# The attention of a fused kernel wholly in plain float32, a pair of heads in two halves of the array

## The chip, the cores and the metric

The kernel runs on one core of one Trainium2 chip. Its time is the device time of one execution in microseconds; the time before is 933.35 us, the median of three runs (932.42 to 933.69).

TensorE multiplies matrices from SBUF into PSUM; each matmul has a weight load, which the profile shows as an engine of its own, PEld. ScalarE (ACT) does activations and copies, VectorE (DVE) elementwise work, and SyncE (SP) issues all transfers.

## The reference

Four batches of 448 rows pass through sigmoid attention (12 heads of 64), then a block with a time shift, a squared ReLU and a gate, then a mixer over rows and channels:

```
scores = q @ k.T / sqrt(64) - log(448)
x   = sigmoid(scores) @ v                      # per head, then the heads side by side: 448 x 768
xk, xr = mu * x + (1 - mu) * x_prev            # x_prev: x shifted by one row
y   = sigmoid(xr @ w_r) * (relu(xk @ w_k)**2 @ w_v)
u   = y + (relu(y.T @ w_tok1) @ w_tok2).T
out = u + relu(u @ w_ch1) @ w_ch2
```

## The kernel before

**Split numbers.** Nearly every product is done on pairs of rounded float32r values. `split` (lines 100 to 105) makes `hi`, a rounded copy (a CAST on ACT or DVE, as the table `ONDVE` says), and `lo = src - hi` (a subtraction on DVE). A product is then three rounded matmuls, hi x hi, hi x lo and lo x hi (`products`, lines 421, 423, 424).

**Attention, per head.** Two heads make a pair, six pairs a batch. `unit_k` and `unit_q` split keys, queries and values of a head. The head dimension is 64, so a K tile holds hi in one half of the 128 rows and lo in the other, and the scores of a chunk of 128 keys are two rounded matmuls over all rows (lines 194, 195), eight for a head. Line 201 is the sigmoid of two chunks. Lines 207 to 215 split it, and the values are seven rounded matmuls (lines 232, 234), with hi and lo of the values side by side in the columns, which line 237 adds.

Twelve heads of the table `NATIVE`, eight in batch 0 and four in batch 1, take the values another way: the sigmoid and the values stay plain float32, and four plain matmuls with 64 columns (line 227) make the head's output; the last has only 64 rows (`TAIL`). `TAIL` is the last chunk of the 448 keys.

**What runs beside what.** Batch 0's attention runs first, with the first weights prepared beside it (after unit number `EARLY`). From then on the units of the next batch's attention stand between the projections: `spread` gives each unit a due time, and `run` takes the units that are due after every two steps of a product. Each weight chunk is loaded, narrowed from float64 on first use (`narrow`, two ACT and two DVE instructions, lines 272 to 281), stored for later use, and split; `w_tick` does so some chunks ahead. A list scheduler then sets the order on each engine by readiness.

**Waits around the units.** `ps_sc` has two buffers of two PSUM banks (scores), `ps_av` one (values). Keys have one buffer, queries, values and plain sigmoids two or three.

Of the kernel before, what the change touches and what calls it, by code (L numbers as in the profile page):

```python
# [9 lines left out]
F32 = mybir.dt.float32  # L10
# [12 lines left out]
P = 128  # L23
# [11 lines left out]
    return ap.bitcast(F32)  # L35


ONDVE = [('K', 0), ('K', 1), ('K', 2), ('K', 3), ('Q', 0), ('Q', 2), ('Q', 3), ('V', 1), ('V', 2), ('kk', 0), ('kk', 3), ('mix', 1), ('mix', 2), ('mix', 3), ('prev', 2), ('sq', 2)]


WARM = 12
END_1 = 1.0
BEG_2 = 0.15
END_2 = 0.65
EARLY = 20

TURNED = 2
TURN = 1
BLK = 32

NATIVE = {(0, 1), (0, 7), (0, 4), (1, 1), (0, 3), (1, 8), (1, 4), (0, 6), (0, 2), (0, 5), (1, 9), (0, 11)}


def native(b, pr, h):
    return (b, 2 * pr + h) in NATIVE


@with_exitstack
def kernel(
# [23 lines left out]
    def pool(name, bufs, **kw):  # L86
        return ctx.enter_context(tc.tile_pool(name=name, bufs=bufs, **kw))
# [2 lines left out]
    wraw, wpool, wsplit = pool("wraw", 3), pool("wpool", 2), pool("wsplit", 3)  # L90
    dram = pool("dram", 1, space=bass.MemoryType.DRAM)
    tmps = pool("tmps", 4)
    a1, a2, a3 = pool("a1", 1), pool("a2", 2), pool("a3", 3)
    ps_mm = pool("ps_mm", 3, space=PSUM)
    ps_av, ps_sc = pool("ps_av", 1, space=PSUM), pool("ps_sc", 2, space=PSUM)

    def ENG(kind, b):
        return DVE if (kind, b) in ONDVE else ACT
# [10 lines left out]

    kns, qns, vns = {}, {}, {}  # L110


    def load_k(g):
        if g < B * NPAIR:
            kns[g] = a1.tile([P, 4 * P], F32, tag="kn", name="kn")
            SP.dma_start(out=kns[g], in_=k[g])

    def load_q(g):
        if g < B * H:
            qns[g] = a2.tile([P, S], F32, tag="qn", name="qn")  # L120
            SP.dma_start(out=qns[g], in_=q[g])

    def load_v(g):
        if g < B * NPAIR:
            vns[g] = a2.tile([P, 2, 4, D], F32, tag="vn", name="vn")
            SP.dma_start(out=vns[g], in_=v[g])


# [7 lines left out]
    for _ in range(WARM):  # L136
        PE.matmul(idle[:, :S], zero[:, :P], zero, start=True, stop=True)

    load_k(0)
    load_q(0)  # L140
    load_v(0)
    load_q(1)

    ident = const.tile([P, P], F32, tag="ident", name="ident")
    make_identity(nc, ident)

    load_v(1)

    mus = {}
    for name, src in (("k", mu_k), ("r", mu_r)):  # L150
# [9 lines left out]

    att = {}

    def unit_k(b, pr, h):
        g = b * NPAIR + pr
        kn = kns[g]
        me = slice(h * D, h * D + D)
        ot = slice(D - h * D, P - h * D)
        K = a3.tile([P, 4 * P], F32R, tag="KK", name="KK")
        split(K[me], K[ot], kn[me], ENG("K", b))
        att[(b, pr, h)] = {"K": K}  # L170

    def unit_q(b, pr, h):
        g = b * NPAIR + pr
        st = att[(b, pr, h)]
        qn = qns.pop(2 * g + h)
        Q1 = a2.tile([P, S], F32R, tag="Q1", name="Q1")
        Q2 = a2.tile([P, S], F32R, tag="Q2", name="Q2")
        split(Q1, Q2, qn, ENG("Q", b))
        st["Q"] = (Q1, Q2)
        vn = vns[g][:, h]  # L180
        if native(b, pr, h):
            st["v"] = vn
        else:
            vs = a3.tile([P, 4, 2 * D], F32R, tag="vs", name="vs")
            split(vs[:, :, 0:D], vs[:, :, D:], vn, ENG("V", b))
            st["v"] = vs

    def unit_qk(b, pr, h, c2):
        st = att[(b, pr, h)]
        K, (Q1, Q2) = st["K"], st["Q"]  # L190
        ps = ps_sc.tile([P, 2, 512], F32, tag="sc", name="psc")
        for j in range(2):
            c = c2 * 2 + j
            PE.matmul(ps[:, j, :S], K[:, c * P : (c + 1) * P], Q1, start=True, stop=False)  # L194
            PE.matmul(ps[:, j, :S], K[:, c * P : (c + 1) * P], Q2, start=False, stop=True)  # L195
        plain = native(b, pr, h)
        if plain:
            a = a3.tile([P, 2, S], F32, tag="al" if c2 else "ah", name="a")
        else:
            a = a2.tile([P, 2, S], F32, tag="a", name="a")  # L200
        ACT.activation(a, ps[:, :, :S], AF.Sigmoid, bias=-math.log(S), scale=1.0 / math.sqrt(D))  # L201
        if plain:
            st[c2] = a
            return
        ah = a3.tile([P, 2, S], F32R, tag="ah", name="ah")
        al = a3.tile([P, 2, S], F32R, tag="al", name="al")
        if ENG("ah", b) is ACT:
            ACT.copy(ah, a)  # L208
        else:
            DVE.tensor_copy(ah, a)  # L210
        if c2 == 0:
            DVE.tensor_tensor(out=al, in0=a, in1=f32(ah), op=ALU.subtract)
        else:
            DVE.tensor_tensor(out=al[:, 0], in0=a[:, 0], in1=f32(ah[:, 0]), op=ALU.subtract)
            DVE.tensor_tensor(out=ah[TAIL:, 1], in0=a[TAIL:, 1], in1=f32(ah[TAIL:, 1]), op=ALU.subtract)  # L215
        st[c2] = (ah, al)

    def unit_av(b, pr, h):
        st = att.pop((b, pr, h))
        vs = st["v"]  # L220
        ps = ps_av.tile([P, 512], F32, tag="av", name="pav")
        me = slice(h * D, h * D + D)
        ot = slice(D - h * D, P - h * D)
        if native(b, pr, h):
            for c in range(4):
                n = P if c < 3 else TAIL
                PE.matmul(ps[:D, :S], vs[:n, c], st[c // 2][:n, c % 2], start=(c == 0), stop=(c == 3))  # L227
            ACT.copy(xe[me, pr, 1:], ps[:D, :S])
            return
        for c in range(4):  # L230
            ah, al = st[c // 2]
            PE.matmul(ps[:, :S], vs[:, c], ah[:, c % 2], start=(c == 0), stop=(c == 3))  # L232
            if c < 3:
                PE.matmul(ps[:, :S], vs[:, c], al[:, c % 2], start=False, stop=False)  # L234
        tmp = tmps.tile([P, S], F32, tag="tmp", name="avt")
        ACT.copy(tmp[me], ps[ot, :S])
        DVE.tensor_tensor(out=xe[me, pr, 1:], in0=ps[me, :S], in1=tmp[me], op=ALU.add)

    def attention_units(b, then=()):

        u = [lambda: unit_k(b, 0, 0), lambda: unit_q(b, 0, 0), lambda: unit_k(b, 0, 1)]
        for pr in range(NPAIR):
            nx = pr + 1 < NPAIR
            u.append(lambda pr=pr: (unit_qk(b, pr, 0, 0), load_q(2 * (b * NPAIR + pr) + 2)))
            if pr == 0:
                u.append(lambda: load_k(b * NPAIR + 1))
            u.append(lambda pr=pr: unit_q(b, pr, 1))
            if pr:
                u.append(lambda pr=pr: (unit_av(b, pr - 1, 1), load_v(b * NPAIR + pr + 1)))
                u += [f[pr - 1] for f in then]  # L250
            u.append(lambda pr=pr: (unit_qk(b, pr, 0, 1), load_q(2 * (b * NPAIR + pr) + 3)))
            if nx:
                u.append(lambda pr=pr: unit_k(b, pr + 1, 0))
            u.append(lambda pr=pr: unit_qk(b, pr, 1, 0))
            u.append(lambda pr=pr: unit_av(b, pr, 0))
            if nx:
                u.append(lambda pr=pr: unit_q(b, pr + 1, 0))
                u.append(lambda pr=pr: unit_k(b, pr + 1, 1))
            u.append(lambda pr=pr, nx=nx: (unit_qk(b, pr, 1, 1), nx and load_k(b * NPAIR + pr + 2)))
        u.append(lambda: (unit_av(b, NPAIR - 1, 1), load_v(b * NPAIR + NPAIR + 1)))  # L260
        u += [f[NPAIR - 1] for f in then]
        return u

# [417 lines left out]
def lay_out(x):  # L681

    import numpy as np

    def chunks(w, parts=1):

        kt = w.shape[0] // (P * parts)
        w = w.reshape(parts, kt, P, w.shape[1] // P, P).transpose(3, 0, 2, 1, 4)
        return w.reshape(-1, P, kt * P)

    qt = x["q"].transpose(0, 1, 3, 2).reshape(B * H, D, S)
    kt = x["k"].transpose(0, 1, 3, 2).reshape(B * NPAIR, P, S)
    v = x["v"].reshape(B * NPAIR, 2, S, D)
    head = v[:, :, : 3 * P].reshape(B * NPAIR, 2, 3, P, D).transpose(0, 3, 1, 2, 4)
    tail = v[:, :, 3 * P :].transpose(0, 2, 1, 3)[:, :, :, None]
    y = {
        "q": np.concatenate([qt, qt], axis=1),
        "k": np.concatenate([kt, kt[:, :, 3 * P :]], axis=2),
        "v": np.concatenate([head, np.concatenate([tail, tail], axis=1)], axis=3),
        "moe_mu_k": x["moe_mu_k"].reshape(NT, P).T,  # L700
        "moe_mu_r": x["moe_mu_r"].reshape(NT, P).T,
        "moe_w_k": chunks(x["moe_w_k"]),
        "moe_w_v": chunks(x["moe_w_v"], 2),
        "moe_w_r": chunks(x["moe_w_r"]),
        "moe2_w_tok1": chunks(np.concatenate([x["moe2_w_tok1"], x["moe2_w_tok1"][3 * P :]])),
        "moe2_w_tok2": x["moe2_w_tok2"],
        "moe2_w_ch1": chunks(x["moe2_w_ch1"]),
        "moe2_w_ch2": chunks(x["moe2_w_ch2"], 2),
    }
    y = {n: np.ascontiguousarray(a) for n, a in y.items()}  # L710

    return {n: a.view(np.int64) if a.dtype == np.float64 else a for n, a in y.items()}
# [41 lines left out]
```

## Time and profile before

| | |
|---|---|
| median of three runs | 933.35 us |
| span of the profiled execution (the page gives no other time for it) | 933.1 us |
| TensorE matmuls busy | 919.8 us, 99% |
| weight loads busy | 803.6 us, 86% |
| VectorE busy | 663.0 us, 71% |
| ScalarE busy | 518.2 us, 56% |
| transfers, share of 16 engines | 46.2% |

A matmul's record lasts longer than the step to the next, since matmuls are pipelined: busy time says that TensorE had work, and the distance of two starts says what a matmul costs. A "128*64" ahead of a matmul's shape is the part of the array that it takes, rows by columns.

### The profile page before, as it was taken

Reading aid. Unit: us, or ns where it says so; the run is one execution under the profiler, and the core shown is the slowest. Engines: PE = TensorE matmul, PEld = TensorE weight load, DVE = VectorE, ACT = ScalarE, POOL = GpSimd, SP = SyncE. Lnnn points to the kernel's source line nnn. Section 1 sums busy time; section 2 is a strip of 40 time slices with the busy share of each in tenths; the row PEclk is TensorE's granted clock in tenths of the full one; section 3 lists DMA queues with packets and bytes.
Section 4 is the critical chain, followed back from the end, with each engine's and each line's share of the span. In section 5 each row is a group of like instructions: output and inputs, shape, how many; then the busy total and the mean of one; then the engine's idle time right before and its main releaser. Section 6 shows DMA issues by size and latency. Waiting matters only on the chain.

```text
span 933.1 us, 12192 instructions
## 1 busy us (share of the span) xinstructions
PE 919.8 (99%) x4448; PEld 803.6 (86%) x4448; DVE 663.0 (71%) x1117; ACT 518.2 (56%) x794; POOL 1.3 (0%) x10
## 2 busy tenths in 40 slices
PE   8999999999999999999999999999999999999998
PEld 3477888789999889899898999999999999898987
DVE  7999999998567998677889379988745552332231
ACT  6998998864665867545641277766444432112210
POOL 0000000000000000000000000000000000000000
PEclk9999999999999999999999999999999999999999
DMA  7844866754446656565534333343335421242131
GB/s 250 274 137 129 291 233 199 229 170 129 117 124 192 228 170 198 174 221 194 171 137 152 130 115 115 107 123 95 109 105 161 126 81 51 81 136 71 51 101 72
DMA packets 63228, 138.77 MB, mean 149 GB/s; under 512 B 12736, under 2 KB 29632, under 8 KB 63168
## 3 DMA queue, kind: packets, MB, share of 16 engines
q1 hardware_dynamic: 63168, 137.99, 46.2%
q8 instruction: 35, 0.57, 0.2%
q14 instruction: 25, 0.20, 0.1%
HBM read 106.96 MB, written 29.62 MB: 146 GB/s over the span
## 4 chain that ended last, share of the span: by engine, by line
PE 86%; DVE 8%; DMA 4%; issue 1%; ACT 1%; SPq 0%; ACTq 0%; DVEq 0%
PE psmm L424 24%; PE psmm L421 24%; PE psmm L423 23%; PE pav L227 4%; PE psc L194 3%; PE psc L195 3%; PE pav L232 2%; DMA raw<-in_moe_w_ch_dram 2%; PE pav L234 2%; DVE wlo L105 1%; DMA raw<-in_moe_w_r_dram 1%; DVE wd L280 1%; DVE wd L277 1%; DMA kn<-in_k_dram 1%; PE psmm L474 1%
## 5 line engine op out<-in xcount | busy, mean ns | idle before, releaser
L424 PE MATMUL psmm<-Ah,wlo 128*128 128x448 f32 (+2 forms) x688 | 248.9, 362 | 0.5 <-DVE wlo L105 0.5
L421 PE MATMUL psmm<-Ah,whi 128*128 128x448 f32 (+2 forms) x688 | 248.8, 363 | 0.0
L102 ACT CAST whi<-wd 128x768 fp32r<-128x768 f32 (+1 forms) x160 | 121.6, 760 | 222.6 <-PE psmm L423 210.4
L423 PE MATMUL psmm<-Al,whi 128*128 128x448 f32 (+2 forms) x672 | 243.5, 362 | 0.1
L105 DVE TENSOR_TENSOR wlo<-wd,whi 128x768 fp32r<-128x768 f32 (+1 forms) x160 | 137.8, 861 | 88.5 <-ACT whi L102 86.3
L421 PE MATMUL psmm<-Mh,whi 128*128 128x448 f32 (+2 forms) x480 | 175.7, 366 | 0.0
L423 PE MATMUL psmm<-Ml,whi 128*128 128x448 f32 (+2 forms) x480 | 174.8, 364 | 0.8 <-DVE Ml L105 0.8
L424 PE MATMUL psmm<-Mh,wlo 128*128 128x448 f32 (+2 forms) x480 | 174.9, 364 | 0.0
L421 PEld LDWEIGHTS psmm<-Ah,whi 128*128 128x128 f32 x688 | 129.2, 188 | 14.2 <-issue 2.8
L424 PEld LDWEIGHTS psmm<-Ah,wlo 128*128 128x128 f32 x688 | 129.2, 188 | 11.6 <-DVE wlo L105 0.9
L423 PEld LDWEIGHTS psmm<-Al,whi 128*128 128x128 f32 x672 | 126.2, 188 | 11.9 <-DVE Al L105 0.8
L201 ACT ACTIVATE a<-psc 128x896 f32<-128x896 f32 x96 | 87.4, 916 | 22.6 <-PE psc L195 22.1
L423 PEld LDWEIGHTS psmm<-Ml,whi 128*128 128x128 f32 x480 | 90.2, 188 | 9.8 <-DVE Ml L105 1.1
L421 PEld LDWEIGHTS psmm<-Mh,whi 128*128 128x128 f32 x480 | 90.2, 188 | 9.3 <-issue 0.7
L424 PEld LDWEIGHTS psmm<-Mh,wlo 128*128 128x128 f32 x480 | 90.1, 188 | 8.6
L195 PE MATMUL psc<-Q,KK 128*128 128x448 f32 x192 | 70.2, 367 | 1.3 <-DVE Q L105 1.3
L194 PE MATMUL psc<-Q,KK 128*128 128x448 f32 x192 | 70.8, 371 | 0.7 <-ACT a L201 0.4
L208 ACT CAST ah<-a 128x896 fp32r<-128x896 f32 x72 | 67.8, 943 | 1.3
L274 ACT ACTIVATE raw<-raw 128x768 uint32<-128x768 uint32 (+2 forms) x54 | 45.5, 842 | 30.8 <-DMA raw<-in_moe_w_ch_dram 25.1
L272 ACT ACTIVATE wd<-raw 128x768 f32<-128x768 f32 (+2 forms) x54 | 45.1, 836 | 20.0 <-DVE wlo L105 16.3
L277 DVE SCALAR_TENSOR_TENSOR wd<-wd,raw 128x768 uint32<-128x768 uint32 (+2 forms) x54 | 46.9, 872 | 10.2 <-ACT wd L272 9.8
L232 PE MATMUL pav<-ah,vs 128*128 128x448 f32 x144 | 53.6, 372 | 0.2 <-DVE ah L215 0.2
(85 smaller groups left out, 1031.1 us busy)
## 6 DMA issues: line engine op xcount, KB each, us to landing
wd<-w SPq DMA_DIRECT2D x66, 384.0 KB, 3.0
raw<-in_moe_w_ch_dram SPq DMA_DIRECT2D x24, 768.0 KB, 5.3
w<-wd SPq DMA_DIRECT2D x38, 384.0 KB, 2.7
qn<-in_q_dram SPq DMA_DIRECT2D x48, 224.0 KB, 3.0
wd<-w SPq DMA_DIRECT2D x42, 256.0 KB, 2.8
kn<-in_k_dram SPq DMA_DIRECT2D x24, 256.0 KB, 2.8
vn<-in_v_dram SPq DMA_DIRECT2D x24, 256.0 KB, 3.8
raw<-in_moe_w_k_dram SPq DMA_DIRECT2D x8, 768.0 KB, 6.6
```

What stands on the lines that cost most here:

```text
L102: ACT.copy(hi, src)
L105: DVE.tensor_tensor(out=lo, in0=src, in1=hi.bitcast(F32), op=ALU.subtract)
L194: PE.matmul(ps[:, j, :S], K[:, c * P : (c + 1) * P], Q1, start=True, stop=False)
L195: PE.matmul(ps[:, j, :S], K[:, c * P : (c + 1) * P], Q2, start=False, stop=True)
L201: ACT.activation(a, ps[:, :, :S], AF.Sigmoid, bias=-math.log(S), scale=1.0 / math.sqrt(D))
L208: ACT.copy(ah, a)
L232: PE.matmul(ps[:, :S], vs[:, c], ah[:, c % 2], start=(c == 0), stop=(c == 3))
L274: ACT.activation(lo, lo, AF.Copy, bias=0.4375, scale=0.875 * 2.0**-29)
L277: DVE.scalar_tensor_tensor(out=dst, in0=dst, scalar=3, in1=lo, op0=ALU.logical_shift_left, op1=ALU.bitwise_or)
L421: PE.matmul(ps[:, :n], wh, xh, start=(i == 0), stop=False)
L423: PE.matmul(ps[:, :n], wh, xl, start=False, stop=False)
L424: PE.matmul(ps[:, :n], wl, xh, start=False, stop=(i == count - 1))
```

## The change

The splits of attention go, and with them `unit_k`, `unit_q`, the table `NATIVE` and its two ways. Keys and queries of a pair lie in one tile each, head 0 in rows 0 to 63 and head 1 in rows 64 to 127. `unit_qk` multiplies, for each chunk of keys, head 0's rows and then head 1's, each into its own PSUM bank, in plain float32, and takes the sigmoid of both heads at once. `unit_av` multiplies, chunk by chunk, head 0's values into rows 0 to 63 of one PSUM bank (the array's first 64 columns) and head 1's into rows 64 to 127 (the last 64), and one copy puts both into `xe`. The values of the last chunk are filled with zeros instead of a copy, so that all four chunks have 128 rows. A pair is three units now, two of scores (two chunks each) and one of values. Keys have two buffers, values three, sigmoids eight.

```
-EARLY = 20
+EARLY = 12
...
+    def unit_qk(b, pr, chunks):
         g = b * NPAIR + pr
+        for c in chunks:
+            ps = ps_sc.tile([P, 2, 512], F32, tag="sc", name="psc")
+            for h in range(2):
+                me = slice(h * D, h * D + D)
+                PE.matmul(ps[:, h, :S], kns[g][me, c * P : (c + 1) * P], qns[g][me], start=True, stop=True)
+            a = a8.tile([P, 2, S], F32, tag="a", name="a")
+            ACT.activation(a, ps[:, :, :S], AF.Sigmoid, bias=-math.log(S), scale=1.0 / math.sqrt(D))
+            att[(g, c)] = a
+
+    def unit_av(b, pr):
         g = b * NPAIR + pr
...
         ps = ps_av.tile([P, 512], F32, tag="av", name="pav")
...
         for c in range(4):
...
+            a = att.pop((g, c))
+            for h in range(2):
+                PE.matmul(ps[h * D : h * D + D, :S], vns[g][:, h, c], a[:, h], start=(c == 0), stop=(c == 3))
+        ACT.copy(xe[:, pr, 1:], ps[:, :S])
...
         for pr in range(NPAIR):
...
+            g = b * NPAIR + pr
+            u.append(lambda pr=pr, g=g: (unit_qk(b, pr, (0, 1)), load_kq(g + 1), load_v(g + 1)))
             if pr:
...
+                u.append(lambda pr=pr: unit_av(b, pr - 1))
                 u += [f[pr - 1] for f in then]
...
+            u.append(lambda pr=pr: unit_qk(b, pr, (2, 3)))
+        u.append(lambda: unit_av(b, NPAIR - 1))
         u += [f[NPAIR - 1] for f in then]
```

The order on TensorE at the start of batch 0, before; `psc` are scores, `pav` values, `KK` and `Q` split keys and queries, `idle` the warming matmuls:

```order
L137 MATMUL idle<-zero 128x448
L194 MATMUL psc<-Q_209,KK 128x448 x2
L195 MATMUL psc<-Q_210,KK 128x448
L194 MATMUL psc<-Q_209,KK 128x448
L195 MATMUL psc<-Q_210,KK 128x448 x2
L194 MATMUL psc<-Q_209,KK 128x448
L195 MATMUL psc<-Q_210,KK 128x448
```

And in the changed kernel, where `kn` and `qn` are the loaded keys and queries, to the end of the first pair's scores and values; a row with x2 is the two heads:

```order
L124 MATMUL idle_98<-zero_96 128x448
L152 MATMUL psc_202<-qn_113,kn_111 128x448 x2
L152 MATMUL psc_207<-qn_113,kn_111 128x448 x2
L152 MATMUL psc_218<-qn_113,kn_111 128x448 x2
L152 MATMUL psc_223<-qn_113,kn_111 128x448 x2
L152 MATMUL psc_228<-qn_214,kn_212 128x448 x2
L152 MATMUL psc_233<-qn_214,kn_212 128x448 x2
L163 MATMUL pav_244<-a_205,vn_115 64x448 x2
L163 MATMUL pav_244<-a_210,vn_115 64x448 x2
L163 MATMUL pav_244<-a_221,vn_115 64x448 x2
L163 MATMUL pav_244<-a_226,vn_115 64x448 x2
L152 MATMUL psc_266<-qn_214,kn_212 128x448 x2
```

No split stands ahead of the scores any more, and batch 0 is now 14 groups of scores and values in turn, with all of its scores but one group ahead of the first projection.

Between the projections of batch 1, before, TensorE had four rounded matmuls of a unit, in the shape of their neighbours (`psmm`, `Ah`, `whi` and so on are projections):

```order
L424 MATMUL psmm<-Ah,wlo 128x448
L194 MATMUL psc<-Q_953,KK 128x448
L195 MATMUL psc<-Q_954,KK 128x448
L194 MATMUL psc<-Q_953,KK 128x448
L195 MATMUL psc<-Q_954,KK 128x448
L421 MATMUL psmm<-Ah,whi 128x448
```

Now it has four plain ones:

```order
L340 MATMUL psmm<-Ah,wlo 128x448
L152 MATMUL psc<-qn,kn 128x448 x4
L337 MATMUL psmm<-Ah,whi 128x448
```

There are 54 such groups in batches 1 to 3 (36 of scores with x4, one of them in two parts, and 18 of values with x8), each between projections.

ScalarE's queue at the start, before; `ah` are roundings of sigmoids, `avt` the copy of one half of the values:

```order
L201 ACTIVATE a<-psc 128x896 x2
L208 CAST ah<-a 128x896 x2
L201 ACTIVATE a<-psc 128x896 x2
L272 ACTIVATE wd<-raw 128x768
L236 COPY avt<-pav 64x448
L274 ACTIVATE raw<-raw 128x768
```

And in the changed kernel; `a` are sigmoids, `wd`, `raw` and `whi` weights, `xe` the value copy, `mix` and `Ah` the scaled and rounded inputs of the projections:

```order
L154 ACTIVATE a<-psc 128x896
L190 ACTIVATE raw<-raw 128x768
L154 ACTIVATE a<-psc 128x896
L188 ACTIVATE wd<-raw 128x768
L190 ACTIVATE raw<-raw 128x768
L93 CAST whi<-wd 128x768
L164 COPY xe<-pav 128x448
L190 ACTIVATE raw<-raw 128x768
L324 ACTIVATE mix_254<-xe,omr 128x448
L154 ACTIVATE a<-psc 128x896
L324 ACTIVATE mix_260<-xe,omk 128x448
L93 CAST Ah<-mix_255 128x448
```

Six sigmoids now stand ahead of the first value copy, and sigmoids, weights and the projections' inputs follow each other in one queue. Up to the last product of batch 0's attention it holds 24 sigmoids, 6 copies, 12 scalings (`mix`), 12 roundings (`Ah`), 13 conversions of weights (5 of line 188, 8 of line 190) and 3 roundings of weights.

## Rows read from the trace of the kernel before

**Rows 1.** The page, part 1: busy us (share) and instructions of each engine.

```profile
PE 919.8 (99%) x4448; PEld 803.6 (86%) x4448; DVE 663.0 (71%) x1117; ACT 518.2 (56%) x794; POOL 1.3 (0%) x10
```

**Rows 2.** Busy time by stretch; columns as in the first line.

```profile
core 0: us, PE busy (x) PEld busy (x) DVE busy (x) ACT busy (x) POOL busy (x), PEclk, DMA share, GB/s
0.00:10.00 10.00, 7.38 (x26) 4.00 (x27) 5.64 (x15) 4.13 (x6) 1.33 (x10) 1.00 0.67 199
10.00:20.00 10.00, 7.98 (x27) 3.80 (x26) 9.10 (x15) 8.41 (x12) 0.00 (x0) 1.00 0.88 298
20.00:30.00 10.00, 10.00 (x32) 4.48 (x32) 9.83 (x16) 9.82 (x15) 0.00 (x0) 1.00 0.86 307
...
150.00:200.00 50.00, 48.20 (x234) 39.63 (x233) 48.86 (x91) 37.52 (x67) 0.00 (x0) 1.00 0.66 208
...
800.00:933.00 133.00, 129.49 (x645) 116.31 (x643) 38.06 (x65) 18.90 (x28) 0.00 (x0) 1.00 0.27 87
```

**Rows 3.** In order of time, TensorE's start: start us, us, instruction, [idle before].

```profile
1.26 3.96 PE L137 MATMUL idle<-zero 128*128 128x448 bf16 x12 [1.26 <-POOL zero L134]
...
5.48 0.67 PE L194 MATMUL psc<-Q,KK 128*128 128x448 f32 x2 [0.26 <-DVE Q L104]
```

**Rows 4.** Line 227 alone: ns min/median/max, first and last start, forms.

```profile
L227 PEld LDWEIGHTS pav<-a,vn x96: 129/137/137, 16.5 to 195.3; 128*64 128x64 f32 x72, 64*64 64x64 f32 x24
L227 PE MATMUL pav<-a,vn x96: 536/539/591, 16.5 to 195.7; 128*64 128x448 f32 x72, 64*64 64x448 f32 x24
```

**Rows 5.** In order of time, one native head and the scores after it.

```profile
20.68 0.37 PE L195 MATMUL psc<-Q,KK 128*128 128x448 f32 x1
...
20.98 3.36 PE L227 MATMUL pav<-a,vn 128*64 128x448 f32 x8
...
21.41 0.14 PEld L227 LDWEIGHTS pav<-a,vn 128*64 128x64 f32 x1 [0.24 <-issue]
...
22.53 0.14 PEld L227 LDWEIGHTS pav<-a,vn 128*64 128x64 f32 x1 [0.24 <-issue]
...
23.37 0.19 PEld L227 LDWEIGHTS pav<-a,vn 64*64 64x64 f32 x2 [0.70 <-issue]
...
24.27 0.47 PE L194 MATMUL psc<-Q,KK 128*128 128x448 f32 x1
...
24.38 0.19 PEld L195 LDWEIGHTS psc<-Q,KK 128*128 128x128 f32 x1
...
24.58 0.36 PE L195 MATMUL psc<-Q,KK 128*128 128x448 f32 x1
...
25.79 0.36 PE L195 MATMUL psc<-Q,KK 128*128 128x448 f32 x1
```

**Rows 6.** Groups by line and shape: busy us, mean ns | idle before.

```profile
L208 ACT CAST ah<-a 128x896 fp32r<-128x896 f32 x72 | 67.8, 943 | 1.3
...
L212 DVE TENSOR_TENSOR al<-a,ah 128x896 fp32r<-128x896 f32 x36 | 39.2, 1088 | 12.2 <-ACT ah L208 11.8
...
L194 PEld LDWEIGHTS psc<-Q,KK 128*128 128x128 f32 x192 | 35.9, 188 | 9.1 <-issue 4.5 <-ACT a L201 0.8 <-DVE Q L104 0.7
```

**Rows 7.** ScalarE's groups of the first 54 us.

```profile
L201 ACT ACTIVATE a<-psc 128x896 f32<-128x896 f32 x18 | 15.9, 914 | 1.8 <-PE psc L195 1.7
L274 ACT ACTIVATE raw<-raw 128x768 uint32<-128x768 uint32 x7 | 6.4, 919 | 0.0
...
L102 ACT CAST Ah<-mix 128x448 fp32r<-128x448 f32 x8 | 4.5, 562 | 0.1
...
L408 ACT ACTIVATE mix<-xe,omk 128x448 f32<-128x448 f32 x4 | 2.7, 664 | 0.0
...
L102 ACT CAST whi<-wd 128x768 fp32r<-128x768 f32 x3 | 2.5, 834 | 0.0
```

**Rows 8.** Transfers: issues, KB each, median us to landing.

```profile
qn<-in_q_dram SPq DMA_DIRECT2D x48, 224.0 KB, 3.0
```

More of the change, by code (lines that the diff above doesn't have):

```diff
@@ L35, in f32 @@
     return ap.bitcast(F32)
-ONDVE = [('K', 0), ('K', 1), ('K', 2), ('K', 3), ('Q', 0), ('Q', 2), ('Q', 3), ('V', 1), ('V', 2), ('kk', 0), ('kk', 3), ('mix', 1), ('mix', 2), ('mix', 3), ('prev', 2), ('sq', 2)]
+ONDVE = [('kk', 0), ('kk', 3), ('mix', 1), ('mix', 2), ('mix', 3), ('prev', 2), ('sq', 2)]
 WARM = 12
@@ L49 @@
 BLK = 32
-NATIVE = {(0, 1), (0, 7), (0, 4), (1, 1), (0, 3), (1, 8), (1, 4), (0, 6), (0, 2), (0, 5), (1, 9), (0, 11)}
-def native(b, pr, h):
-    return (b, 2 * pr + h) in NATIVE
 @with_exitstack
@@ L92 @@
     tmps = pool("tmps", 4)
-    a1, a2, a3 = pool("a1", 1), pool("a2", 2), pool("a3", 3)
+    a2, a3, a8 = pool("a2", 2), pool("a3", 3), pool("a8", 8)
     ps_mm = pool("ps_mm", 3, space=PSUM)
@@ L110, with load_kq @@
     kns, qns, vns = {}, {}, {}
-    def load_k(g):
+    def load_kq(g):
         if g < B * NPAIR:
-            kns[g] = a1.tile([P, 4 * P], F32, tag="kn", name="kn")
+            kns[g] = a2.tile([P, 4 * P], F32, tag="kn", name="kn")
             SP.dma_start(out=kns[g], in_=k[g])
-    def load_q(g):
-        if g < B * H:
             qns[g] = a2.tile([P, S], F32, tag="qn", name="qn")
@@ L124, in load_v @@
         if g < B * NPAIR:
-            vns[g] = a2.tile([P, 2, 4, D], F32, tag="vn", name="vn")
+            vns[g] = a3.tile([P, 2, 4, D], F32, tag="vn", name="vn")
             SP.dma_start(out=vns[g], in_=v[g])
@@ L137 @@
         PE.matmul(idle[:, :S], zero[:, :P], zero, start=True, stop=True)
-    load_k(0)
-    load_q(0)
+    load_kq(0)
     load_v(0)
-    load_q(1)
     ident = const.tile([P, P], F32, tag="ident", name="ident")
     make_identity(nc, ident)
-    load_v(1)
     mus = {}
@@ L161 @@
     att = {}
-    def unit_k(b, pr, h):
+    def unit_qk(b, pr, chunks):
         g = b * NPAIR + pr
[L165 to L172, printed above, removed]
-        g = b * NPAIR + pr
[L174 to L216, printed above, removed]
@@ L218, in unit_av @@
-    def unit_av(b, pr, h):
-        st = att.pop((b, pr, h))
-        vs = st["v"]
-        ps = ps_av.tile([P, 512], F32, tag="av", name="pav")
[L222 to L229, printed above, removed]
-        for c in range(4):
[L231 to L237, printed above, removed]
+        for c in chunks:
[6 more added lines that the diff above has]
+            att[(g, c)] = a
@@ L239, in attention_units @@
+    def unit_av(b, pr):
+        g = b * NPAIR + pr
+        ps = ps_av.tile([P, 512], F32, tag="av", name="pav")
+        for c in range(4):
+            a = att.pop((g, c))
+            for h in range(2):
+                PE.matmul(ps[h * D : h * D + D, :S], vns[g][:, h, c], a[:, h], start=(c == 0), stop=(c == 3))
+        ACT.copy(xe[:, pr, 1:], ps[:, :S])
     def attention_units(b, then=()):
-        u = [lambda: unit_k(b, 0, 0), lambda: unit_q(b, 0, 0), lambda: unit_k(b, 0, 1)]
+        u = []
@@ L242, in attention_units @@
         for pr in range(NPAIR):
[L243 to L247, printed above, removed]
+            g = b * NPAIR + pr
+            u.append(lambda pr=pr, g=g: (unit_qk(b, pr, (0, 1)), load_kq(g + 1), load_v(g + 1)))
             if pr:
-                u.append(lambda pr=pr: (unit_av(b, pr - 1, 1), load_v(b * NPAIR + pr + 1)))
+                u.append(lambda pr=pr: unit_av(b, pr - 1))
@@ L250, in attention_units @@
                 u += [f[pr - 1] for f in then]
[L251 to L259, printed above, removed]
@@ L260, in attention_units @@
-        u.append(lambda: (unit_av(b, NPAIR - 1, 1), load_v(b * NPAIR + NPAIR + 1)))
+            u.append(lambda pr=pr: unit_qk(b, pr, (2, 3)))
+        u.append(lambda: unit_av(b, NPAIR - 1))
         u += [f[NPAIR - 1] for f in then]
@@ L689, in chunks @@
         return w.reshape(-1, P, kt * P)
-    qt = x["q"].transpose(0, 1, 3, 2).reshape(B * H, D, S)
+    qt = x["q"].transpose(0, 1, 3, 2).reshape(B * NPAIR, P, S)
     kt = x["k"].transpose(0, 1, 3, 2).reshape(B * NPAIR, P, S)
@@ L696, in lay_out @@
     y = {
-        "q": np.concatenate([qt, qt], axis=1),
+        "q": qt,
         "k": np.concatenate([kt, kt[:, :, 3 * P :]], axis=2),
-        "v": np.concatenate([head, np.concatenate([tail, tail], axis=1)], axis=3),
+        "v": np.concatenate([head, np.concatenate([tail, np.zeros_like(tail)], axis=1)], axis=3),
         "moe_mu_k": x["moe_mu_k"].reshape(NT, P).T,
```

## The prediction

> **What bounds the kernel now.** I read the page's busy times first. TensorE's matmuls are busy 919.8 us of a span of 933.1, VectorE 663.0, ScalarE 518.2 [rows 1]. So TensorE is idle for 13.3 us only. The table of stretches says where: 2.6 and 2.0 us in the first two tens (1.26 of it before the first warming matmul [rows 3]), 3.5 at the end, and the 5.2 that are left are spread over the rest, 1.8 of them at 150 to 200, where VectorE is busy for 48.9 of 50; the granted clock is 1.00 in each [rows 2]. The middle of the program, where projections and attention share TensorE, is thus TensorE's, and an edit is worth there what it adds to or takes from TensorE. In the first 54 us the other two are as full as TensorE: from 20 to 30 all three are busy 9.8 or more of 10 [rows 2]. So the change is priced in two places, batch 0 (attention alone) and batches 1 to 3 (attention between projections).
>
> **The price of TensorE's pieces.** The view of line 227 gives 96 records to its 48 plain float32 matmuls, two passes for each, in two forms [rows 4]; the order of time gives their pace. Weight loads inside a group come at 21.41 to 22.53, three steps of 0.373 us, so a pass is 0.373 and a plain matmul 0.746 [rows 5]. A rounded matmul (lines 194, 195) goes every 0.202 us, from 24.58 to 25.79 in six steps. The same rows price a change of the array's shape. Into the group: 20.68 to 20.98, 0.30 where 0.20 is usual, so 0.10. Between the group's own two forms: eight passes are 2.98 and the group takes 3.29, and the weight load of the second form stands idle for 0.70 where 0.24 is usual; I split the 0.31 evenly, 0.15 here and 0.15 at the way out. After it, the first rounded matmul takes 0.31 to the next in place of 0.20, so 0.11 more. In and out is 0.36, and a whole native head (line 227) costs 0.10 + 3.29 + 0.11 = 3.5 us.
>
> Before, for a head: scores 8 x 0.202 = 1.62, values 7 x 0.202 = 1.41 where split and 3.5 where native. Batches 1 to 3 have 36 heads, 4 of them native: 58.2 + 32 x 1.41 + 14.0 = 117.4 us. Batch 0 has 12, 8 of them native: 19.4 + 5.7 + 28.0 = 53.1.
>
> **What the change adds.** All passes become plain ones: per pair and chunk two matmuls for scores and two for values, four passes each. No row of before has two matmuls in different parts of the array, so the cost of a pair of passes lies between 0.373 us (side by side) and 0.746 (one after the other). I take side by side with matmuls starting in program order. In that order head A's two passes come before head B's two, so B starts one pass late: A at 0 and 0.373, B at 0.373 and 0.746, A again at 0.746. A unit is its passes side by side and one pass more. I take this end because the operands of the two heads lie in other rows or columns, and because weight loads are no limit: the first rounded matmul's load goes with it at 24.27 and the next load starts at 24.38, 0.11 us on [rows 5], and the time of a pass must hold two.
>
> A score unit is 4 x 0.373 + 0.373 + 0.36 = 2.22 us, a value unit 8 x 0.373 + 0.373 + 0.36 = 3.72. The new order of TensorE has 54 such units in batches 1 to 3, each between rounded matmuls, so each pays both changes; before, only the 12 native groups did. 18 pairs x (2 x 2.22 + 3.72) = 146.9, that is **+29.5**. One after the other it would be 18 x (2 x 3.34 + 6.33) = 234, +117.
>
> **Batch 0.** Before, its 53.1 us start at 5.48 [rows 3], and of the 4.6 us of idle time in the first 20 us 3.4 come after the warming matmuls' start: about 62.0, the last of it between projections. After, TensorE needs 96 passes side by side, 35.8 us, 14 late heads of 0.373 and 14 changes of about 0.15, 43.1 in all, and would end at 48.6. But ScalarE does not allow it. Its queue now holds, up to the last product of batch 0: 24 sigmoids at 0.914, 12 scalings at 0.664, 12 roundings at 0.562 and 6 copies at about the same, and for the weights 13 conversions at 0.919 and 3 roundings at 0.834 [rows 7]: 54.4 us. The first sigmoid waits for three passes from 5.48, to 6.6; the last stands a copy, two scalings and two roundings, 3.0, before the end of that work, at 58.0, and the last values need 1.1 more: 59.1. **-3** (between -13, were ScalarE not there, and +3, were it idle for 6 us in between).
>
> **What goes.** VectorE loses every split of keys, queries, values and scores (line 212 alone 36 x 1088 ns = 39.2), ScalarE the 72 roundings of line 208, 67.8 us [rows 6]. Beside a TensorE that is the bound this returns only TensorE's idle time between 20 and 800 us, 5.2 at most [rows 2]: I take **-4**, bounds -5.2 and 0. The query loads are halved, 24 of 224 KB instead of 48; with the keys double buffered they are asked for a pair ahead, about 7 us, against a landing of 3.0 [rows 8], and cost nothing; late, one of them would cost those 3 once. They stand on the same queue ahead of the weights' loads, which `w_raw(i + 6)` asks for chunks ahead. The sigmoids stay 96 of the same shape. The value copy is one of 128 rows for a pair and waits on ScalarE's queue with the sigmoids behind it; the single buffer it frees is next needed two score units later.
>
> Sum: 933.1 + 29.5 - 3 - 4 = 955.6, and the median of the runs, 933.35, is 0.25 over the span: **956 us**.
>
> [...] The loads at 21.41 to 22.53 run while a matmul in the same rows runs: each stands idle for 0.24, loads for 0.14, and the passes still go every 0.373 [rows 5]. [...]
>
> No row shows when a second head may start. If it starts with the first, the late pass of each unit goes: 54 x 0.373 = 20.1 us of the sum, and **936** is left (batch 0 stays with ScalarE); with all of the 5.2 us of idle time gone, 934.6, level with before. [...] I hold against it that each matmul is two passes here, which must follow each other: 10%.
>
> **Rivals.** (1) The overlap is partial. If a weight load must wait its turn behind the matmul ahead of it in the queue, B's first load starts only when A's second pass does: two passes and two loads in a row per chunk, 0.746 + 2 x 0.188 = 1.12 for scores [rows 6] and 0.746 + 2 x 0.137 = 1.02 for values [rows 4]. Units are then 2.79 and 4.68, 184.7 for 18 pairs, +67; batch 0 about level: **996**. If only the row halves overlap, 18 x (2 x 2.22 + 6.33) = 194, and about **1008**. For it: in every row a load starts only with the matmul before it. Against: there it needs the same rows, which B's does not.
> (2) No overlap, the change does not do what it says: +117, and batch 0 takes 71.6 + 2.1 from 5.3, to 79, +17: 933.1 + 117 + 17 - 4 + 0.3 = **1063**. For it: no row shows overlap.
> (3) The other side: nothing drains or waits around a unit, because the first head's passes of one unit run beside the last matmuls of the work ahead. The place is the ends of the 54 units, the price the late pass and the changes, 0.73 us each, 39.6 in all: **916**. It decides from 0.27 us per unit downwards, where the time falls under 931. Against: the 0.36 is measured, on a shape of the same width as the values'.
>
> **How the numbers follow.** Forecast 40% (942 to 972: bounds of batch 0 and the idle time, and 0.1 us more or less per unit); rival 1 23% (985 to 1020); rival 2 13% (1045 to 1080); both heads at once 10% (931 to 940), half of it within 0.2%, 1.9 us, which is about what a measurement of this kernel can tell; rival 3 14% (912 to 931). Faster 14%, same 5%, slower 81%. The range 925 to 1030 holds the forecast, rival 1, both heads at once and a third of rival 3, near 80%.
>
> **What would show it.** In the profile after, the start times of the score matmuls tell: records of the two heads at the same pace as one (eight passes of a score unit in about 1.9 us) for the forecast, in 2.4 for rival 1, in 3.0 for rival 2, in 1.5 for both heads at once. The gap from a unit's last pass to the second rounded matmul after it shows the change of shape. ScalarE should be busy 9.5 or more of 10 up to about 58 us with TensorE waiting for it, and TensorE full from there. A TensorE that idles on ScalarE or VectorE in batches 1 to 3, or a granted clock that falls in the half-filled units, would make all of this wrong.

## The result, and the profile after

The changed kernel takes 941.53 us (median of four runs, 939.16 to 945.28) against 933.52 for the kernel before: ratio 1.0091, 95% interval 1.0065 to 1.0117. Slower, as forecast, but by 8 us and not by 22.5.

The page of the kernel after, busy times and granted clock [rows 1]:

```profile
PE 924.4 (98%) x4484; PEld 732.8 (78%) x4484; DVE 458.7 (49%) x737; ACT 428.4 (45%) x670; POOL 1.3 (0%) x10
...
PEclk9899999999999999999999999999999999999999
```

VectorE lost 204 us of work and ScalarE 90, and the kernel got slower: over most of the program TensorE bounds it. The profiled execution has a span of 943.2, 10.1 over before's. It is the longest run, that of 945.28; in all four runs the time is 2.0 to 2.2 us over the span, not 0.25 as I took it. In the runs of the kernel before that stand beside the experiments it is 1.8 over; if that holds for its 933.1 too, that was a run longer than the median.

One score unit and one value unit of batch 1, TensorE in order of time [rows 5]:

```profile
65.30 0.37 PE L340 MATMUL psmm<-Ah,wlo 128*128 128x448 f32 x1
65.60 1.77 PE L152 MATMUL psc<-qn,kn 64*128 64x448 f32 x8
67.30 0.47 PE L337 MATMUL psmm<-Ah,whi 128*128 128x448 f32 x1
67.61 0.36 PE L339 MATMUL psmm<-Al,whi 128*128 128x448 f32 x1
...
152.36 0.37 PE L340 MATMUL psmm<-Mh,wlo 128*128 128x448 f32 x1
152.65 3.23 PE L163 MATMUL pav<-a,vn 128*64 128x448 f32 x16
155.81 0.47 PE L337 MATMUL psmm<-Mh,whi 128*128 128x448 f32 x1
156.12 0.36 PE L339 MATMUL psmm<-Ml,whi 128*128 128x448 f32 x1
```

From the last rounded matmul ahead to the second one behind, less two regular steps of 0.202, a score unit costs 67.61 - 65.30 - 0.40 = 1.91 us and a value unit 156.12 - 152.36 - 0.40 = 3.36 (the same to 0.1 in nearly all of 54). That is 4 and 8 passes of 0.373 and 0.4 (0.42 and 0.38) for the change of shape: the two heads run side by side from their first pass. The first score unit shows it directly, in a narrow stretch, matmuls and weight loads:

```profile
5.85 1.02 PE L152 MATMUL psc<-qn,kn 64*128 64x448 f32 x4
...
5.85 0.30 PEld L152 LDWEIGHTS psc<-qn,kn 64*128 64x128 f32 x4 [0.73 <-issue]
6.33 0.19 PEld L152 LDWEIGHTS psc<-qn,kn 64*128 64x128 f32 x2 [0.18 <-issue]
```

Four passes are over after 1.02 us, the time of two passes and the end of the last; loads come in twos, and the trace has the two heads' passes start 6 or 7 ns apart.

Batch 0, by stretch [rows 2]:

```profile
10.00:20.00 10.00, 6.62 (x32) 2.27 (x32) 5.14 (x6) 8.89 (x13) 0.00 (x0) 0.97 0.78 275
20.00:30.00 10.00, 9.90 (x34) 3.26 (x36) 6.12 (x9) 9.02 (x14) 0.00 (x0) 0.68 0.65 251
30.00:40.00 10.00, 7.98 (x32) 2.28 (x30) 5.91 (x9) 9.01 (x14) 0.00 (x0) 1.00 0.96 335
40.00:50.00 10.00, 8.27 (x32) 2.72 (x32) 2.18 (x5) 7.22 (x12) 0.00 (x0) 0.83 0.48 169
50.00:60.00 10.00, 8.29 (x32) 2.71 (x32) 2.35 (x4) 5.76 (x9) 0.00 (x0) 0.83 0.22 74
```

Here the granted clock falls to a mean of 0.68 and 0.83; before, it was 1.00 throughout. TensorE waits for sigmoids, and the clock is low after the longer waits: 0.50 from 20.1 to 26.0 us, after 3.48 us up to 20.10; 0.50 from 44 to 46, after 1.45 and 0.71 up to 41.02 and 42.76; 0.50 from 54 to 56, after 0.99 and 0.71 up to 51.28 and 53.02. From 30 to 40, with no wait over 0.80 us, it is 1.00. Loads of the score and value units around 20 to 27 us:

```profile
20.10 3.69 PE L152 MATMUL psc<-qn,kn 64*128 64x448 f32 x8 [3.48 <-ACT a L154]
...
24.52 0.23 PEld L163 LDWEIGHTS pav<-a,vn 128*64 128x64 f32 x2 [0.51 <-issue]
25.26 0.23 PEld L163 LDWEIGHTS pav<-a,vn 128*64 128x64 f32 x2 [0.51 <-issue]
26.01 0.23 PEld L163 LDWEIGHTS pav<-a,vn 128*64 128x64 f32 x2 [0.51 <-issue]
26.54 0.14 PEld L163 LDWEIGHTS pav<-a,vn 128*64 128x64 f32 x2 [0.30 <-issue]
26.92 0.14 PEld L163 LDWEIGHTS pav<-a,vn 128*64 128x64 f32 x2 [0.24 <-issue]
```

After 3.48 us of waiting a pass takes 0.745 us, at the granted clock of 0.50; from 26.5 on 0.375, at 1.00 (26.5 to 28.0).

**Where the 10.1 us of span are.** Before, the first projection starts at 53.15, but a part of batch 0's attention still stands between the projections that follow, 33 rounded matmuls and one whole native head:

```profile
53.15 0.36 PE L421 MATMUL psmm<-Ah,whi 128*128 128x448 f32 x1
...
70.52 3.36 PE L227 MATMUL pav<-a,vn 128*64 128x448 f32 x8
```

Of the 96 records of line 227, 40 start after 53.15, and batch 1's four native heads have only 32 of them. At 0.202 and 3.5 us, batch 0's attention takes TensorE up to 53.15 + 6.7 + 3.5 = 63.3. After, all of it stands ahead of the first projection, at 64.2: +0.9. Batches 1 to 3 cost 117.4 us by the same prices before; after, 18 x (2 x 1.91 + 3.36) = 129.2: +11.8. What is left of the span was 752.4 and is 749.8: -2.6. Sum +10.1.

The -2.6 is a remainder and no row shows it as a whole. TensorE's idle time behind the first projection is a small part of it: 5.1 us before (53.15 to 929.5), 4.2 after (64.18 to 939.5). More comes from the attention itself, whose pieces before, many of them single matmuls between projections, cost some 4 us more over their price, by the starts around them, than the units of the kernel after do over theirs. Against it stands a stretch at a granted clock of 0.50 in batch 1 (187 to 189 us): TensorE waits 2.09 us for VectorE up to 185.47, and from 186.8 to 189.8 a rounded matmul goes every 0.37 us in place of 0.20; the mean clock is 0.66 from 186 to 191, 1.7 us in all.

### The profile page after: what moved, and what is told of

Same layout as the page of the kernel before. It is cut to its first block, busy times and chain, and to the rows that moved or that the text cites. A ratio compares the mean times of both kernels' runs of the same rounds, so it can differ in the third digit from the quotient of the medians.

```text
span 943.2 us, 11702 instructions
## 1 busy us (share of the span) xinstructions
PE 924.4 (98%) x4484; PEld 732.8 (78%) x4484; DVE 458.7 (49%) x737; ACT 428.4 (45%) x670; POOL 1.3 (0%) x10
## 4 chain that ended last, share of the span: by engine, by line
PE 74%; DMA 12%; ACT 6%; DVE 5%; issue 2%; SPq 1%; ACTq 0%; DVEq 0%
PE psmm L337 21%; PE psmm L340 21%; PE psmm L339 20%; PE pav L163 6%; DMA raw<-in_moe_w_ch_dram 5%; PE psc L152 5%; DMA raw<-in_moe_w_v_dram 2%; ACT wd L188 2%; DMA raw<-in_moe_w_r_dram 2%; ACT a L154 1%; DVE wd L193 1%; DVE wlo L96 1%; DVE wd L196 1%; DMA raw<-in_moe_w_k_dram 1%; ACT whi L93 1%
## 5 line engine op out<-in xcount | busy, mean ns | idle before, releaser
L337 PE MATMUL psmm<-Ah,whi 128*128 128x448 f32 (+2 forms) x688 | 253.0, 368 | 0.4 <-DVE Ml L460 0.3
L337 PE MATMUL psmm<-Mh,whi 128*128 128x448 f32 (+2 forms) x480 | 177.8, 370 | 0.0
L337 PEld LDWEIGHTS psmm<-Ah,whi 128*128 128x128 f32 x688 | 129.2, 188 | 36.2 <-issue 19.9
L340 PEld LDWEIGHTS psmm<-Ah,wlo 128*128 128x128 f32 x688 | 129.2, 188 | 10.8
L152 PE MATMUL psc<-qn,kn 64*128 64x448 f32 x384 | 90.1, 578 | 10.2 <-ACT a L154 10.2
L154 ACT ACTIVATE a<-psc 128x896 f32<-128x896 f32 x96 | 84.7, 909 | 21.0 <-PE psc L152 21.0
L163 PE MATMUL pav<-a,vn 128*64 128x448 f32 x384 | 82.7, 569 | 0.3 <-ACT a L154 0.3
L190 ACT ACTIVATE raw<-raw 128x768 uint32<-128x768 uint32 (+2 forms) x54 | 45.2, 837 | 65.4 <-DMA raw<-in_moe_w_ch_dram 47.4
L152 PEld LDWEIGHTS psc<-qn,kn 64*128 64x128 f32 x384 | 33.0, 188 | 50.7 <-issue 23.9
L163 PEld LDWEIGHTS pav<-a,vn 128*64 128x64 f32 x384 | 26.6, 143 | 48.1 <-issue 44.3
```

The source lines that it names most:

```text
L152: PE.matmul(ps[:, h, :S], kns[g][me, c * P : (c + 1) * P], qns[g][me], start=True, stop=True)
L163: PE.matmul(ps[h * D : h * D + D, :S], vns[g][:, h, c], a[:, h], start=(c == 0), stop=(c == 3))
L190: ACT.activation(lo, lo, AF.Copy, bias=0.4375, scale=0.875 * 2.0**-29)
L337: PE.matmul(ps[:, :n], wh, xh, start=(i == 0), stop=False)
L340: PE.matmul(ps[:, :n], wl, xh, start=False, stop=(i == count - 1))
```

## The experiments

Each kernel was timed beside the kernel before on the same chip; ratios are to that.

**e1, the order inside a unit.**

```
-        for c in range(4):
-            for h in range(2):
+        for h in range(2):
+            for c in range(4):
                 PE.matmul(ps[h * D : h * D + D, :S], vns[g][:, h, c], ...)
```

> The changed kernel with the order of the matmuls inside a unit turned: all chunks of head 0, then all of head 1 (a value unit is four matmuls of the first column half, then four of the second). Theory: TensorE takes a pass of the other half as soon as that half is free, whatever stands between them in program order; value units stay at 3.36 us and the time near 941. Rival: passes start in program order and only a neighbour runs beside its neighbour; then head 1 starts with head 0's last pass, a value unit takes 15 x 0.373 + 0.41 = 6.0 us, 18 of them add 47 us, and with the score units (7 passes, 3.0 us, where they stand in turn) the time is 990 to 1030.

967.78 us, ratio 1.0382 (1.0368 to 1.0396). Score units, turned in the same way, stay at 1.91; value units take 4.91: neither 3.36 nor 6.0. The weight loads of a value unit, in order of time:

```profile
84.10 0.19 PEld L164 LDWEIGHTS pav<-a,vn 128*64 128x64 f32 x2 [0.30 <-issue]
84.53 0.14 PEld L164 LDWEIGHTS pav<-a,vn 128*64 128x64 f32 x1 [0.24 <-issue]
84.91 0.14 PEld L164 LDWEIGHTS pav<-a,vn 128*64 128x64 f32 x1 [0.24 <-issue]
85.29 0.14 PEld L164 LDWEIGHTS pav<-a,vn 128*64 128x64 f32 x1 [0.24 <-issue]
85.66 0.19 PEld L164 LDWEIGHTS pav<-a,vn 128*64 128x64 f32 x3 [0.24 <-issue]
```

Head 0 loads alone; at 85.66, when its fifth pass starts and three of its eight still wait, head 1's first load goes too. 4.91 is 12 passes and the change of shape: head 1 starts four passes late. So neither theory: in this unit TensorE takes a pass for the free half past three waiting ones, at 85.66, and not past the four to seven that wait before. The score units agree: there a head has four passes, three wait when its first one runs, and the other head starts at once.

**e8, the same with three and three.** To test "past at most three waiting passes":

```
+        for h, c in ((0, 0), (0, 1), (0, 2), (1, 0), (1, 1), (1, 2), (0, 3), (1, 3)):
```

> As e1, values alone: three matmuls of head 0, three of head 1, then one of each (scores in the changed kernel's order). Theory, from e1's 4.91 us: TensorE takes a pass for the free half past at most three waiting passes of the busy one. Then head 1 starts when head 0's third pass does, two passes late, nothing else waits, and a value unit takes 10 x 0.373 + 0.36 = 4.1 us; 18 units add 13 us: 950 to 957. Rival: it looks past matmuls only from the neighbour on (head 1 starts with head 0's last waiting pass): 13 x 0.373 + 0.36 = 5.2 us a unit and 965 or more.

955.20 us, ratio 1.0235 (1.0219 to 1.0250), value units 4.16. As the theory said, two passes of head 0 go alone at the start and two of head 1 at the end, the first three loads of a unit and the last two:

```profile
83.14 0.19 PEld L162 LDWEIGHTS pav<-a,vn 128*64 128x64 f32 x2 [0.30 <-issue]
83.57 0.14 PEld L162 LDWEIGHTS pav<-a,vn 128*64 128x64 f32 x1 [0.24 <-issue]
83.95 0.20 PEld L162 LDWEIGHTS pav<-a,vn 128*64 128x64 f32 x3 [0.24 <-issue]
...
85.89 0.14 PEld L162 LDWEIGHTS pav<-a,vn 128*64 128x64 f32 x1 [0.24 <-issue]
86.26 0.14 PEld L162 LDWEIGHTS pav<-a,vn 128*64 128x64 f32 x1 [0.24 <-issue]
```

**e2, no halves for the scores.**

```
-            kns[g] = a2.tile([P, 4 * P], ...)
+            kns[g] = a2.tile([D, 2, 4 * P], ...)     # loaded as "(h d) n -> d h n"; queries likewise
-                PE.matmul(ps[:, h, :S], kns[g][me, ...], qns[g][me], ...)
+                PE.matmul(ps[:, h, :S], kns[g][:, h, ...], qns[g][:, h], ...)
```

> The changed kernel with both heads' keys and queries in rows 0 to 63, so that all score matmuls take the same row half. Theory: the pair runs side by side because of the two halves; without them a score unit takes 8 x 0.373 + 0.41 = 3.4 us in place of 1.91, 36 of them add 54 us, batch 0 some more (its scores take 17.9 us instead of 9 per 24 matmuls, partly beside ScalarE): 995 to 1012. Rival: a plain matmul over 64 rows is simply faster than one over 128, half or no half: near 941.

992.83 us, ratio 1.0654 (1.0633 to 1.0674), 2 us under the theory's range. A score unit, with its neighbours:

```profile
65.94 0.37 PE L339 MATMUL psmm<-Ah,wlo 128*128 128x448 f32 x1
66.24 3.27 PE L151 MATMUL psc<-qn,kn 64*128 64x448 f32 x8
69.44 0.47 PE L336 MATMUL psmm<-Ah,whi 128*128 128x448 f32 x1
69.74 0.36 PE L338 MATMUL psmm<-Al,whi 128*128 128x448 f32 x1
```

69.74 - 65.94 - 0.40 = 3.40 us against 1.91, as the theory has it: the halves are what makes the pair run at once, and they are worth 51 us here. The kernel shows something else besides, in its first 64 us and those of the kernel after, each in one stretch:

```profile
0.00:64.00 64.00, 62.46 (x202) 25.17 (x204) 25.09 (x36) 47.76 (x67) 1.33 (x10) 1.00 0.73 222
```

```profile
0.00:64.00 64.00, 53.01 (x204) 17.22 (x204) 24.54 (x36) 47.38 (x67) 1.33 (x10) 0.89 0.64 224
```

Batch 0 has 48 score matmuls, 96 passes: one after the other they take 35.8 us, 17.9 more than side by side. With this TensorE is hardly ever idle, the clock stays at 1.00 and the first projection starts at 64.82, not 64.18. So of batch 0's time in the kernel after, some 17 us are TensorE waiting or running at a granted clock of 0.50; its rows have 9.5 us less busy time and a mean clock of 0.89, which is worth 7 of the 64 us. ScalarE is busy for 47.4 of 64 us: it does not fill batch 0.

**e3, e7: relief of ScalarE in batch 0.**

```
+ONDVE = [('mix', 0), ('prev', 0), ...               # e3
+ONDVE = [('mix', 0), ('prev', 0), ('low', 0), ...   # e7: also line 190, one conversion of each weight chunk, in all batches
```

> The changed kernel with batch 0's 12 scalings and 12 roundings of the projections' inputs moved from ScalarE to VectorE, which is 20 to 60% busy there. Theory: batch 0 is held by ScalarE's queue, and the granted clock falls because TensorE waits for it; with 14.7 us less on ScalarE the first projection starts at 50 to 54 us in place of 64.2, the clock stays at full, and the time is 928 to 932, below the kernel before. Rival: batch 0 is held by the weights' loads or by TensorE itself: 938 or more.

> The changed kernel with batch 0's scalings and roundings on VectorE as in e3, and with one of the two ScalarE conversions of each weight chunk (line 190, 54 x 0.84 us over the whole program, 8 of them in batch 0) on VectorE too. Theory: what still holds batch 0 after e3 is ScalarE's queue, where sigmoids stand behind conversions that wait for weights; with them gone the first projection starts at 50 to 55 us (58.97 in e3), the granted clock stays up, and the time is 928 to 933. Rival: batch 0 waits for something else (loads, VectorE): 935 to 938, as e3.

e3: 936.49 us, ratio 1.0039 (1.0027 to 1.0052), first projection at 58.97. e7: 932.63, ratio 0.9996 (0.9986 to 1.0006), first projection at 53.87. e3 fell between theory and rival; e7, with weights' conversions out of the sigmoids' way too, came out as the theory has it, by its start of the projections and the upper end of its time. 10.3 us earlier there, 8.9 us in the whole (not all of it need be batch 0's, since line 190 is moved everywhere). So ScalarE did hold batch 0, but through the order of its queue. In the kernel after, ScalarE behind a value unit, and the score unit that waits:

```profile
48.64 0.53 ACT L164 COPY xe<-pav 128x448 f32<-128x448 f32 x1 [2.75 <-PE pav L163]
49.20 0.67 ACT L324 ACTIVATE mix<-xe,omr 128x448 f32<-128x448 f32 x1
49.77 0.65 ACT L324 ACTIVATE mix<-xe,omk 128x448 f32<-128x448 f32 x1
50.33 0.90 ACT L154 ACTIVATE a<-psc 128x896 f32<-128x896 f32 x1
...
51.28 1.02 PE L152 MATMUL psc<-qn,kn 64*128 64x448 f32 x4 [0.99 <-ACT a L154]
```

ScalarE waits for the values and then does the copy and two scalings ahead of the sigmoid for which TensorE waits: they wait for each other in turn.

**e4, more work for TensorE in batch 0.**

```
+                for _ in range(2 if b == 0 else 1):
                     PE.matmul(ps[:, h, :S], ...)
```

> The changed kernel with every score matmul of batch 0 issued twice into the same place: 24 x 0.75 = 18 us more for TensorE at full clock, and no more for any other engine. Theory: in batch 0 TensorE waits for ScalarE, and its clock falls for want of work; the doubled matmuls fill the waits and hold the clock, so the time moves by no more than 941 to 947 and the granted clock up to 64 us rises. Rival: TensorE's own work sets batch 0's end: 956 to 960.

960.39 us, ratio 1.0307 (1.0291 to 1.0323): 0.4 us over the rival's range. The doubled matmuls stand ahead of the waits and not in them: TensorE still waited for sigmoids (up to 3.35 us at a time), the granted clock was 0.82 to 0.84 from 10 to 40, and the first projection came at 79.87. From 50 to 80, at 1.00, TensorE was busy for 9.25 or more of 10, so there its own work did set the pace. e2 gives TensorE the same 17.9 us and fills the waits with them; the scheduler ordered the queues anew in each, and which part of that order makes the difference was not tested.

**e5, the price of a change of shape.**

```
-                u.append(lambda pr=pr: unit_av(b, pr - 1))
+                u.append(lambda pr=pr: (unit_av(b, pr - 1), unit_qk(b, pr, (2, 3))))
```

> The changed kernel with each value unit directly ahead of the next two chunks' score unit, one due time for both: 18 times, TensorE goes from column halves to row halves without rounded matmuls between. Theory: a change of the array's shape costs about 0.2 us at each side, so 18 changes fewer give 18 x 0.25 = 4 to 5 us: 936 to 938. Rival: the changes overlap with the last passes and are not worth it, or the longer block makes other work late: 940 or more.

947.33 us, ratio 1.0150 (1.0137 to 1.0163): a miss. The joined unit does cost less, 86.77 - 81.31 - 0.40 = 5.06 us for 3.36 + 1.91 = 5.27, so here a change from half to half saves 0.2 against going through the whole array; 15 such units in batches 1 to 3, not 18, make 3 us in all. The first projection, at 59.87, is 4.3 earlier, too. Both are lost elsewhere: from 100 to 150 TensorE is busy for 44.1 of 50, where it was 49.2. TensorE's longest wait there, and ScalarE ahead of it:

```profile
142.35 0.74 PE L338 MATMUL psmm<-Mh,whi 128*128 128x448 f32 x1 [3.63 <-ACT whi L93]
...
140.33 0.65 ACT L191 ACTIVATE raw<-raw 128x512 uint32<-128x512 uint32 x1 [4.00 <-DMA raw<-in_moe_w_v_dram]
140.89 0.90 ACT L154 ACTIVATE a<-psc 128x896 f32<-128x896 f32 x1
141.69 0.61 ACT L93 CAST whi<-wd 128x512 fp32r<-128x512 f32 x1
```

ScalarE's queue stands 4 us behind a weight load, and the rounding that TensorE waits for stands in it. That the joined units move that load is likely; it was not tested apart.

**h1, h2, c1, c2: halves only where TensorE is not the bound.** h1 is the kernel before with batch 0 in halves and with the relief of e7 for batch 0:

```
-EARLY = 20
+EARLY = 12
...
+NATIVE = {(1, 1), (1, 8), (1, 4), (1, 9)}        # h2: set()
...
+ONDVE = [..., ('mix', 0), ('prev', 0), ...
+        if not low:                              # narrow: VectorE for the first eight weight chunks
-    for i, unit in enumerate(attention_units(0, [...])):
+    for i, unit in enumerate(half_units([...])):
```

> The kernel before with batch 0 alone done in halves and relieved as in e7 (the conversion only for the first eight weight chunks), batches 1 to 3 split as before with the four native heads of batch 1. Theory: the halves lose where TensorE is the bound (7.2 us for a pair against 6.05) and win only where ScalarE and VectorE are; so this takes the gain of batch 0, where the attention ended near 61 us before and should end at 50 to 55, and none of the loss: 922 to 928. Rival: what batch 0 gains is given back to VectorE's queue in batch 1: 931 or more.

> h1 with the four native heads of batch 1 split too. A native head costs TensorE 3.5 us, a split one 1.41, so TensorE is asked for 8.4 us less, VectorE for some 14 us more in batch 1. Theory: TensorE bounds batch 1 once batch 0 is out of the way: 4 to 8 us under h1. Rival: VectorE bounds it: h1's time or more.

> The kernel before with h1's relief of ScalarE alone: batch 0's scalings and roundings and one conversion of the first eight weight chunks on VectorE, attention as before. Theory: h1 gains by the halves, since before VectorE is as full as ScalarE in batch 0; moving work to it makes it slower: 936 or more. Rival: the relief is what helps h1, halves or not: 925 to 930.

> h1 without the relief: batch 0 in halves as in the changed kernel, batches 1 to 3 split as before. Theory: batch 0 in halves with ScalarE's queue as the change left it ends about 3 us later than before (64.2 against 61.3), and the rest is as before: 933 to 938; halves and relief help only together. Rival: VectorE, free in batch 0, works ahead for batch 1, and the halves help alone: 930 or less.

| kernel | batch 0 | relief | us | ratio to before (95%) |
|---|---|---|---|---|
| before | split and native | no | 932.44 to 932.79 | |
| c1 | split and native | yes | 938.83 | 1.0068 (1.0055 to 1.0080) |
| c2 | halves | no | 929.72 | 0.9967 (0.9954 to 0.9979) |
| h1 | halves | yes | 924.57 | 0.9909 (0.9891 to 0.9927) |
| h2, no native heads in batch 1 | halves | yes | 928.75 | 0.9960 (0.9947 to 0.9974) |

h1 beats both kernels, by 0.9% and 1.8%. The relief alone makes the kernel before slower by 6 us, as expected, since there VectorE is full in batch 0; with the halves it is worth 5. The halves alone gained 3, against the theory and in the rival's range: batch 0's attention ends at 62.14, 1.2 us before the 63.3 of the kernel before (the theory's 61.3 left out the native head that stands behind), and from 100 to 150 and from 300 to 350 TensorE is busy for all of 50 us, where it had 49.22 and 48.84. Busy times of c2 there:

```profile
100.00:150.00 50.00, 50.00 (x241) 43.84 (x240) 47.67 (x81) 44.76 (x73) 0.00 (x0) 1.00 0.54 181
300.00:350.00 50.00, 50.00 (x257) 45.70 (x256) 49.01 (x80) 39.19 (x60) 0.00 (x0) 1.00 0.64 216
```

h2 is the rival's: with the four heads split, 4 us slower, TensorE busy 44.93 of 50 from 150 to 200 (48.38 in h1) at a mean clock of 0.93. There TensorE waits for VectorE, 2.9 us at once for split keys, while VectorE is busy for 47.8 of 50: the four native heads spare VectorE there.

## Why the prediction was wrong

- **The place and the sign** were right: TensorE bounds batches 1 to 3, their units cost more than the splits they replace, and 204 us less on VectorE return little. The sign had a thin margin: without the late pass my sum is +2.4, not +22.5.
- **"B starts one pass late"** is the step that failed, the largest by size: 54 x 0.373 = 20.1 us of the +29.5 that I took. Measured: +11.8. I argued that head A's second pass stands ahead of head B's first in program order and gave both heads at once 10%; in e1 and e8 TensorE took a pass for the free half past three waiting ones (at 85.66 and 83.95), and with two passes per matmul, heads in turn, the units' 1.91 and 3.36 have no late pass in them. That rival had 936; it was the nearest.
- **The change of shape**: 0.36 assumed, 0.42 and 0.38 measured (1.91 and 3.36 less 4 and 8 passes). Right, and e5 shows that it holds between halves too, smaller.
- **Batch 0**: -3 forecast, +0.9 measured, and both ends were off. Before, its attention ended at 63.3 and not at 62.0; after, at 64.2 and not at 59.1. ScalarE's sum of 54.4 us was too large (47.4 busy in 64 us: instructions in a row start closer than their records are long, 49.20 to 49.77 for one of 0.67), and its queue was not full; instead TensorE and ScalarE waited for each other, and TensorE ran at a granted clock of 0.50 after its longer waits (5.9 us of it behind the 3.48). I had named a falling clock as what would prove the sum wrong, and put no price on it.
- **What goes**: -4 forecast, -2.6 measured as a remainder, and not by the way that I gave: of TensorE's 5.1 us of idle time behind the first projection 4.2 are left.
- With heads at once, my own terms make a span of 935.5; of the 7.7 us from there to 943.2, 3.9 are batch 0, 1.4 what goes, and 2.4 the units' change of shape.
- Rivals 1 and 2 (less overlap) and 3 (no cost around a unit) are refuted by the units' 1.91 and 3.36.
- My argument for the late start was that matmuls keep their program order, and e1 and e8 contradict it between halves, by value units of 4.91 and 4.16 us.

## What to carry to other kernels

Two plain matmuls on two halves of the array did run at once here (starts 6 or 7 ns apart in the first score unit), so a pair in plain float32 costs TensorE a fifth more than the three-product split (7.2 us for a pair of heads against 6.05), and the other engines no splits: use it in stages where those bound, and the split where TensorE does (h1, 924.57 us, against 941.53 with halves everywhere). Keep the halves' matmuls alternating (3.36 us for a value unit, against 4.16 and 4.91 in e8 and e1). Each stay costs 0.4 us for going in and out (0.42 and 0.38), which speaks for long groups, but e5's longer ones lost more than they saved (947.33 us). When work leaves an engine, look at what then waits in the queue of the one that is left: here a wait of TensorE of 3.48 us cost the wait and then 5.9 us at a granted clock of 0.50.

## What the runs showed of the hardware

- Plain float32 matmuls of 448 columns were two passes of 0.373 us, on a row half or a column half alike, and two halves ran side by side for both kinds of halves (eight score passes in 1.91 us against 3.40 on one half in e2; 16 value passes in 3.36, where one native head of before took 3.5 for eight).
- A pass for a free half overtook three waiting passes of the other and not four (e1's loads from 84.10 to 85.66): a value unit takes 3.36 us with the heads in turn one matmul each, 4.16 with three (e8), 4.91 with four (e1).
- In the four runs of the changed kernel the span is longer where the granted clock is lower: spans of 937.1, 938.1, 940.8 and 943.2 us at mean clocks of 0.996, 0.995, 0.993 and 0.991.
